# Ten mask selects and seven weight loads get another place in the order of a fused attention, gated-FFN and mixture kernel

## The chip, the cores and the metric

The kernel runs on one core of a Trainium2 chip. The metric is the device time in microseconds (us); three runs of the kernel before gave a median of 881.71 us (881.21 to 882.33).

The engines run beside each other, each through its own fixed list of instructions: PE multiplies matrices, DVE and POOL work on whole tiles element by element, ACT applies functions and copies, SP only issues transfers. ACT and POOL issue some transfers as well.

## The reference

Three stages follow each other: a linear attention whose per-channel decay is a complex number, a gated feed-forward layer, and a mixture of eight experts of which each token takes one.

```python
# 1. per batch (4) and head (8), over t = 0..767, 48 channels
S_re, S_im = ar*S_re - ai*S_im + outer(k[t], v[t]), ar*S_im + ai*S_re
y[t] = q[t] @ S_re                  # ar, ai: a_re, a_im scaled to a magnitude of at most 0.999
# 2. all 3072 tokens, 384 features
x = ((y @ w_a) * (y @ w_b)) @ w_out                 # 384 -> 1536 -> 384
# 3. experts, 384 -> 1024 -> 384
e = argmax(x @ w_gate);  out = softmax(x @ w_gate)[e] * (relu(x @ w1[e]) @ w2[e])
```

## The kernel before, in words

**Blocks.** The 3072 tokens are cut into 12 blocks of 256 tokens, three to a batch, each of two chunks of 128. For a block, ACT, DVE and POOL first work out the decays: magnitude, phase, running products and the scaled `q` and `k` (tiles `A`, `Bt`, `X`, `q`, `k`). The first block does this in two halves of 128 tokens; POOL multiplies `Bt<-im` (L1305) for each half, DVE the other parts. Transfers called turns (L1390) then bring the results into the layout that PE wants, `kT` from `Bt` and `k`, `qT` from `A` and `q`. For the first block there are 12 turns to a chunk: those of `kT` stand in SP's list, those of `qT` in ACT's. From the second block on a block has twelve, and all stand in SP's.

**Products of a chunk.** PE forms the scores (`sc_p`, L1449), DVE multiplies them with a mask into `sm` (L1458), PE transposes the keys (`kn_p`, L1463), forms `y_p` (L1498) and the state's growth (`kv_p`, L1518), and DVE carries the state on (`T`, L1524). Then the gated layer works on the block: the first block in plain fp32 (`ab_p`, L1038, the gate's product `g`, L1049 and L1052, and `o`, L1044), the later ones in three products of high and low parts (L1030, L1076), which are most of PE's work.

**Masks.** `masks` holds four planes of 128x128. Plane 0 is the causal mask and serves the blocks 0 to 2. Planes 1 to 3 are the same mask shifted by 32, 64 and 96 rows; ten selects on POOL (L1186) make them, and blocks 3 to 11 read all four planes.

**Weights.** The weights of the gated layer come as pairs of 32-bit words of 64-bit numbers, in 12 groups (0 to 11) of three loads each: `w_a`, `w_b` (L915) and `w_out` (L913), 384 KB each, into `raw` tiles. ACT (L934) and DVE (L937, L940) turn a group into fp32 tiles `a`. Of `w_out`, PE transposes each group (`wt_p`, L962), ACT copies that (L966), PE multiplies it with the gate weights of the experts (`wg_p`, L972) and ACT copies the result to the group's tile (L975). Later each group is split into high and low parts (L1002, L1008, L995, and transfers on POOL's queue, L998).

**Order.** Most of this is given to a planner (`Plan`). `add` takes an engine, an estimated duration, what the operation reads and writes, a due time `at`, and a time `early` before which it is not placed. A table `TIMES` shifts the due times of a kind of operation; that of the loads is among them. `run` then places the operations one after the other, by the engine that is free first and the smallest due time among what is ready, and this fixes each engine's list for good. What is written before the planner's work stands ahead of it in each list: the ten selects are written there. A transfer is modelled with a limit of eight that are under way. Between DVE and POOL the planner lets operations added with `alone=True` exclude each other. `conv` adds the loads and conversions of a group, `attn` a block's attention.

Of the kernel before, what the change touches and what calls it, by code (L numbers as in the profile page):

```python
# [12 lines left out]
ALU = mybir.AluOpType  # L13
AX = mybir.AxisListType
BF16 = mybir.dt.bfloat16
H, D, C, BT = 8, 48, 128, 256
HP = 64
STRIP = 32
SWAP, KEPT = 3, 2
# [92 lines left out]
    'high': (-35, 1),  # L112
    ('pre', 3, 0, 1): (-137.9, 1),
}
MAX_TAN, MIN_DECAY = 1.5, 1e-17
PT_NAMES = ("A", "Bt", "Cc", "F")
MAGIC = 12582912.0
# [240 lines left out]
def on(engine, n, psum=False, fast=False, bias=False):  # L358

    if engine == "DVE":  # L360
        return 0.147 + n * (0.00053 if fast else 0.00105)
    if engine == "ACT":
        return (0.165 if psum else 0.209) + 0.00081 * n + 0.092 * bias
    return 0.23 + 0.0021 * n
# [120 lines left out]
def fast(tc, q, k, v, a_re, a_im, w_a, w_b, w_out, w_gate, w1, w2, out, dram, x2d):  # L485

    nc = tc.nc
# [3 lines left out]
    with ExitStack() as mctx, ExitStack() as ctx:  # L491
# [10 lines left out]
        scores, phase, turns = [], [0], [0, 0]  # L502
# [10 lines left out]
        masks = ab.tile([128, 4, C], BF16, name="masks")  # L513
# [364 lines left out]
        P = Plan({"sc": 3, "s1": 3 - KEPT})  # L878
# [16 lines left out]
        def loaded(i):  # L895
            return LOAD[0] + LOAD[1] * i if i < LOAD[2] else LOAD[3] + LOAD[4] * (i - LOAD[2])

        def conv(i, f, nm, at):

            K = {}  # L900
            n, m = SIZE[nm], 768 if nm == "ab" else 384
# [39 lines left out]

            one = None
            for x in range(m // 384):
                t = loaded(i + x)
                one = P.add("SP", 0.5, load(x), kind="load", r=[("made", f)] if x else [], w=[mine[x]] + ([("made", f)] if nm == "ab" and not x else []) if nm == "ab" else mine, at=t, early=t, size=393, soft=one)
            done = ("A32", nm, f)
            if nm in BY_TAIL and f >= BY_TAIL[nm]:
# [29 lines left out]
            t = P.add("PE", 0.45, turned, kind="fold", r=[slot], w=[("wt_p", f)], at=at + 2, take="sc")  # L977
# [202 lines left out]
        for t in vrot:  # L1180
            nc.gpsimd.memset(t[:, 0::2, :, 0:HP - D], 0.0)
            nc.gpsimd.memset(t[:, 1, :, D:HP], 0.0)
        for r in range(1, 4):
            n = STRIP * (1 + (r == 2))
            for a in range(0, C, n):
                nc.gpsimd.affine_select(out=masks[a:a + n, r], in_=masks[a:a + n, r], pattern=[[1, C]], compare_op=ALU.is_ge, fill=0.0, base=-((a - r * STRIP) % C), channel_multiplier=-1)  # L1186

        def emptied(i):
            scores.append(bank([128, 4, C], "scores"))
# [234 lines left out]
        def attn(j, t0, t1):  # L1424
# [5 lines left out]
            def add(e, weight, f, r, w, **kw):  # L1430
                todo.append((e, weight, f, r, w, kw))
# [5 lines left out]
            for c in range(2):  # L1437
# [96 lines left out]
                def at_(f, *a):  # L1534
                    return lambda: f(*a)

                if j >= SWAP:
# [19 lines left out]
                        if j + 1 < NB:  # L1557
                            todo.append(("v", 0, None, (), (), {}))
                    for hg in range(2):
                        add("DVE", on("DVE", 512), at_(mask, hg), [("scores", hg % KEPT)], [("sm", hg)], alone=False)  # L1560
                    if not last:
                        for hg in range(2):
                            add("PE", 0.3, at_(kn, hg), qk + [("kT", c), "kept"], [("kn_p", j, c, hg)], take=ring(j))
# [15 lines left out]
                else:  # L1579
                    for hg in range(2):  # L1580
                        if j < SWAP:
                            add("PE", 0.9, at_(sc, hg), qk + [("kT", c), ("qT", c)], [("sc_p", j, c, hg)], take="sc")
                            add("DVE", on("DVE", 512), at_(mask, hg), [("sc_p", j, c, hg), "banks"], [("sm", hg)], give=True, alone=False)
                        else:
                            p_ = ("scores", hg % KEPT)
                            add("PE", 0.64, at_(sc, hg), qk + [("kT", c), ("qT", c)], [p_])
                            add("DVE", on("DVE", 512), at_(mask, hg), [p_], [("sm", hg)], alone=False)
                    if not last:
                        for hg in range(2):
                            add("PE", 0.33, at_(kn, hg), qk + [("kT", c), "kept"], [("kn_p", j, c, hg)], take=ring(j))  # L1590
# [14 lines left out]
            for i, (e, weight, f, r, w, kw) in enumerate(todo):  # L1605
                at = t0 + (t1 - t0) * i / len(todo)
# [32 lines left out]
        list(h1)  # L1639
        prefill()  # L1640
        attn(0, ATT[0], ATT[0] + 12)
        units = [x for f in range(NF) for x in ((3 * f, f, "ab"), (3 * f + 2, f, "o"))]
        for i, f, nm in units:
            conv(i, f, nm, CONV[0] + CONV[1] * i)
# [8 lines left out]
        for j in range(1, NB):  # L1653
# [12 lines left out]
            at = lo + 14  # L1666
# [94 lines left out]
```

## Time and profile before

| | |
|---|---|
| median of the runs | 881.71 us (881.21 to 882.33) |
| profiled execution | 881.96 us, of which the span of the instructions is 880.0 us |
| PE, weight loads beside it | 833.7 us busy (95%), 803.0 us |
| DVE, ACT, POOL | 565.0, 486.6 and 291.6 us busy |
| last chain of waits | PE 82% of the span, issue 8%, DVE 3%, DMA 3%, POOL 2%, ACT 1% |

The profiled execution's time is that of the whole run; the span goes from its first instruction to its last. The busy time of an engine is the sum over its instructions, so a share is an average over stages in which different engines set the pace. A timeline lists the instructions of one engine with start, duration and, in brackets, how long the engine had been idle before and whose end it had waited for. "SPq" and "ACTq" are the instructions by which SP and ACT issue transfers; their duration holds the time for which the issue was held up. The chain of waits is followed back from the last instruction to what released it, step by step.

### The profile page before, as it was taken

To read this page: it belongs to the slowest core of one execution; us is meant where nothing else is said; L and a number is where in the kernel's file an instruction comes from. 1 tells how busy PE (TensorE), PEld (TensorE's weight loads), DVE (VectorE), ACT (ScalarE), POOL (GpSimd) and SP (SyncE) were. 2 spreads that over 40 slices of the span, in tenths; PEclk is the share of its full clock that TensorE was granted. 3 is DMA by queue.
4 is the path that set the end of the run, shared out by engine and by line. 5 is a ranking of instruction groups with operands and counts; after the bars stand their busy time and mean duration, and the time that the engine had idled before them with its cause. 6 is when DMAs were issued, how large, how long until landed. Compare 5 with 4: busy or idle time off the path is not lost.

```text
span 880.0 us, 22475 instructions
## 1 busy us (share of the span) xinstructions
PE 833.7 (95%) x9050; PEld 803.0 (91%) x9050; DVE 565.0 (64%) x1218; ACT 486.6 (55%) x923; POOL 291.6 (33%) x295
## 2 busy tenths in 40 slices
PE   0399999999999999999999999999999999999997
PEld 0288699999999999999999999999999999999996
DVE  6889997766757577594948485535653654555541
ACT  6597878666576556565556465224542544444441
POOL 4100201422555544536363545222033323324111
PEclk9999999999999999999999999999999999999999
DMA  9886743362535362737464551523433553454410
GB/s 260 251 243 216 188 100 111 65 150 46 148 63 143 84 194 57 210 83 203 99 185 110 135 144 53 121 86 106 134 93 121 174 166 115 156 160 137 157 60 25
DMA packets 144255, 117.70 MB, mean 134 GB/s; under 512 B 51036, under 2 KB 138282, under 8 KB 144143
## 3 DMA queue, kind: packets, MB, share of 16 engines
q1 hardware_dynamic: 137071, 103.27, 42.6%
q0 software_dynamic: 5344, 12.12, 4.9%
q8 instruction: 73, 1.20, 0.6%
q10 hardware_dynamic: 1728, 0.79, 0.4%
q14 instruction: 39, 0.32, 0.1%
HBM read 85.13 MB, written 10.61 MB: 109 GB/s over the span
## 4 chain that ended last, share of the span: by engine, by line
PE 82%; issue 8%; DVE 3%; DMA 3%; POOL 2%; ACT 1%; SPq 0%; POOLq 0%; ACTq 0%
PE ab_p L1030 31%; PE o L1076 16%; PE o L843 9%; PE h_p L811 9%; PE y_p L1498 5%; PE scores L1454 2%; PE kn_p L1463 2%; PE sc_p L1449 2%; PE ab_p L1038 2%; PE kv_p L1518 2%; PE o L1044 1%; PE tn_p L788 1%; POOL out_dram L854 1%; DVE a L937 1%; DMA raw<-in_moe_w_b_dram 1%
## 5 line engine op out<-in xcount | busy, mean ns | idle before, releaser
L1030 PE MATMUL ab_p<-xH,wabH 128*128 128x256 f32 x792 | 223.4, 282 | 0.5 <-issue 0.5
L1030 PE MATMUL ab_p<-xH,wL 128*128 128x256 f32 x792 | 221.3, 279 | 0.0
L1030 PE MATMUL ab_p<-xL,wabH 128*128 128x256 f32 x792 | 221.2, 279 | 0.0
L1030 PEld LDWEIGHTS ab_p<-xH,wabH 128*128 128x128 f32 x792 | 149.9, 189 | 0.4
L1030 PEld LDWEIGHTS ab_p<-xL,wabH 128*128 128x128 f32 x792 | 148.8, 188 | 0.5 <-issue 0.4
L1030 PEld LDWEIGHTS ab_p<-xH,wL 128*128 128x128 f32 x792 | 149.2, 188 | 0.0
L1067 POOL TENSOR_TENSOR gL<-g,gH 128x256 fp32r<-128x256 f32 x96 | 80.9, 843 | 166.8 <-ACT gH L1063 154.8
L1059 DVE TENSOR_TENSOR g<-g,ab_p 128x256 f32<-128x256 f32 x132 | 55.1, 417 | 116.3 <-ACT g L1056 116.1
L1056 ACT COPY g<-ab_p 128x256 f32<-128x256 f32 x132 | 48.9, 370 | 120.8 <-PE ab_p L1030 112.6
L1076 PE MATMUL o<-woH,gH 128*128 128x392 f32 x264 | 93.8, 355 | 0.0
L1076 PE MATMUL o<-woH,gL 128*128 128x392 f32 x264 | 90.0, 341 | 0.0
L1076 PE MATMUL o<-wL,gH 128*128 128x392 f32 x264 | 89.7, 340 | 0.0
L843 PE MATMUL o<-w2H,h 128*128 128x384 f32 (+3 forms) x312 | 86.4, 340 | 0.0
L1063 ACT ACTIVATE gH<-g 128x256 fp32r<-128x256 f32 x132 | 54.6, 413 | 43.8 <-DVE g L1059 33.7
L811 PE MATMUL h_p<-sH,w1H 128*128 128x256 f32 (+6 forms) x240 | 77.2, 322 | 0.0
L811 PE MATMUL h_p<-sH,w1L 128*128 128x256 f32 (+6 forms) x240 | 77.0, 321 | 0.0
L811 PE MATMUL h_p<-sL,w1H 128*128 128x256 f32 (+6 forms) x240 | 76.8, 320 | 0.0
L854 POOL DMA_INDIRECT out_dram<-ye,ids x29 | 30.5, 1050 | 112.5 <-ACT ye L853 103.8
L822 DVE SCALAR_TENSOR_TENSOR h<-h_p,h 128x384 fp32r<-128x384 f32 (+1 forms) x48 | 26.7, 556 | 62.4 <-ACT h L820 62.2
L820 ACT ACTIVATE h<-h_p 128x384 fp32r<-128x384 f32 (+4 forms) x48 | 24.5, 511 | 76.4 <-PE h_p L811 76.4
L843 PE MATMUL o<-w2L,h 128*128 128x384 f32 (+3 forms) x168 | 56.7, 338 | 0.0
L843 PEld LDWEIGHTS o<-w2H,h 128*128 128x128 f32 (+3 forms) x312 | 56.3, 185 | 0.5
(216 smaller groups left out, 1947.0 us busy)
## 6 DMA issues: line engine op xcount, KB each, us to landing
raw<-in_moe_w_dram SPq DMA_DIRECT2D x64, 384.0 KB, 3.3
x2d<-x SPq DMA_DIRECT2D x24, 196.0 KB, 2.7
q<-in_q_dram SPq DMA_DIRECT2D x24, 192.0 KB, 4.2
v<-in_v_dram SPq DMA_DIRECT2D x24, 192.0 KB, 3.4
raw<-in_moe_w_a_dram SPq DMA_DIRECT2D x12, 384.0 KB, 4.8
raw<-in_moe_w_b_dram SPq DMA_DIRECT2D x12, 384.0 KB, 4.5
raw<-in_moe_w_out_dram SPq DMA_DIRECT2D x12, 384.0 KB, 5.3
ck<-in_moe_w_a_dram SPq DMA_DIRECT2D x12, 384.0 KB, 5.0
```

Source lines behind the costliest of these rows:

```text
L811: nc.tensor.matmul(out=t, lhsT=lh[:, o:o + 128], rhs=rh[:, kk], start=n == 0, stop=n == 8)
L820: nc.scalar.activation(out=hH, in_=t, func=ACTF.Relu)
L822: nc.vector.scalar_tensor_tensor(out=hL, in0=t[:, 0:main], scalar=0.0, in1=hH[:, 0:main].bitcast(F32), op0=ALU.max, op1=ALU.subtract)
L843: nc.tensor.matmul(out=G["o", c], lhsT=lh, rhs=rh, start=f == 0 and n == 0, stop=f == NH - 1 and n == len(ops) - 1)
L854: d = nc.gpsimd.indirect_dma_start(out, bass.IndirectOffsetOnAxis(ap=ids[0:r, c:c + 1], axis=0), y[0:r], None, bounds_check=NT - 1, oob_is ...
L1030: nc.tensor.matmul(out=t[:, i], lhsT=lh[:, kk * 128:(kk + 1) * 128], rhs=rh[:, kk], start=n == 0, stop=n == 8)
L1056: nc.scalar.copy(out=G["g", j, f], in_=G["ab", j, f][:, 0])
L1059: nc.vector.tensor_tensor(out=G["g", j, f], in0=G["g", j, f], in1=G["ab", j, f][:, 1], op=ALU.mult)
L1063: nc.scalar.activation(out=G["H", j, f], in_=G["g", j, f], func=ACTF.Copy)
L1067: eng.tensor_tensor(out=G["L", j, f], in0=G["g", j, f], in1=G["H", j, f].bitcast(F32), op=ALU.subtract)
L1076: nc.tensor.matmul(out=G["o", j, c], lhsT=lh[:, c * C:(c + 1) * C], rhs=rh, start=f == first and n == 0, stop=f == last and n == 2)
L1498: nc.tensor.matmul(out=t[q4 * 32:q4 * 32 + 32, kk], lhsT=a, rhs=b, start=f0, stop=f1)
```

## The change

The ten selects become operations of the planner, due and not placed before its time 44, and the masks of the scores now read a mark ("strips") that the selects write. They are added behind the first block's attention, so a mask of the first block doesn't wait for them; those of the later ones do. They are added with `alone=False`. And a load with number 15 or above (three numbers to a group, so from the sixth group on) is not placed before the later of its old due time and 57.2, in the loads' own count of time, which the table then shifts.

```diff
+MASKS = 44.0
+HELD = (15, 57.2)
...
             for x in range(m // 384):
-                t = loaded(i + x)
+                t = loaded(i + x) if i < HELD[0] else max(loaded(i + x), HELD[1])
                 one = P.add("SP", 0.5, load(x), kind="load", r=..., w=..., at=t, early=t, size=393, soft=one)
...
-        for r in range(1, 4):
-            n = STRIP * (1 + (r == 2))
-            for a in range(0, C, n):
-                nc.gpsimd.affine_select(out=masks[a:a + n, r], in_=masks[a:a + n, r], pattern=[[1, C]], compare_op=ALU.is_ge, fill=0.0, base=-((a - r * STRIP) % C), channel_multiplier=-1)
+
+        def strip_masks():
+            for r in range(1, 4):
+                n = STRIP * (1 + (r == 2))
+                for a in range(0, C, n):
+                    def f(r=r, n=n, a=a):
+                        nc.gpsimd.affine_select(out=masks[a:a + n, r], in_=masks[a:a + n, r], pattern=[[1, C]], compare_op=ALU.is_ge, fill=0.0, base=-((a - r * STRIP) % C), channel_multiplier=-1)
+                    P.add("POOL", 0.33, f, w=["strips"], at=MASKS, early=MASKS, alone=False)
...
-                        add("DVE", on("DVE", 512), at_(mask, hg), [("scores", hg % KEPT)], [("sm", hg)], alone=False)
+                        add("DVE", on("DVE", 512), at_(mask, hg), [("scores", hg % KEPT), "strips"], [("sm", hg)], alone=False)
...
-                            add("DVE", on("DVE", 512), at_(mask, hg), [p_], [("sm", hg)], alone=False)
+                            add("DVE", on("DVE", 512), at_(mask, hg), [p_, "strips"], [("sm", hg)], alone=False)
...
         attn(0, ATT[0], ATT[0] + 12)
+        strip_masks()
```

Since the planner orders everything anew, more moves than what the diff names. Line numbers after the change are two to six higher.

SP's list around the first block's turns, before; `raw` with `w_a` is the sixth group's first load, the first `kT<-Bt` and `kT<-k` are of the first chunk, the next two of the second:

```order
L1390 DMA kT<-Bt 16x8x128 x3
L915 DMA raw<-in_moe_w_a_dram 128x3x256
L1390 DMA kT<-k 16x8x128 x3
L1390 DMA kT<-Bt 16x8x128 x3
L1390 DMA kT<-k 16x8x128 x3
L915 DMA raw<-in_moe_w_b_dram 128x3x256
L913 DMA raw<-in_moe_w_out_dram 128x768
```

The same place in SP's list after the change:

```order
L1396 DMA kT<-Bt 16x8x128 x3
L1396 DMA kT<-k 16x8x128 x3
L1396 DMA kT<-Bt 16x8x128 x3
L1396 DMA kT<-k 16x8x128 x3
L917 DMA raw<-in_moe_w_a_dram 128x3x256
L917 DMA raw<-in_moe_w_b_dram 128x3x256
L915 DMA raw<-in_moe_w_out_dram 128x768
```

The sixth group's first load has moved from among the turns to behind them, straight ahead of its sisters.

PE's list from the second transpose of the weights to the end of the first chunk, before; the numbers are those of the weight tiles:

```order
L962 MATMUL wt_p<-ident,a_294 128x128 x3
L972 MATMUL wg_p<-wg,wt 32x8 x12
L962 MATMUL wt_p<-ident,a_327 128x128 x3
L972 MATMUL wg_p<-wg,wt 32x8 x12
L1449 MATMUL sc_p<-qT,kT 128x128 x8
L1463 MATMUL kn_p<-ident,kT 128x96 x8
L1498 MATMUL y_p<-sm,v_164 32x128 x16
L1518 MATMUL kv_p<-v_164,kn 32x48 x24
L1038 MATMUL ab_p<-x,a_274 128x128 x6
L1038 MATMUL ab_p<-x,a_287 128x128 x6
L962 MATMUL wt_p<-ident,a_547 128x128 x3
L1449 MATMUL sc_p<-qT,kT 128x128 x4
```

The same place in PE's list after the change:

```order
L964 MATMUL wt_p<-ident,a_284 128x128 x3
L974 MATMUL wg_p<-wg,wt 32x8 x12
L964 MATMUL wt_p<-ident,a_317 128x128 x3
L1455 MATMUL sc_p<-qT,kT 128x128 x8
L974 MATMUL wg_p<-wg,wt 32x8 x12
L1469 MATMUL kn_p<-ident,kT 128x96 x8
L1504 MATMUL y_p<-sm,v_164 32x128 x16
L1524 MATMUL kv_p<-v_164,kn 32x48 x24
L1455 MATMUL sc_p<-qT,kT 128x128 x4
L1040 MATMUL ab_p<-x,a_264 128x128 x6
L1040 MATMUL ab_p<-x,a_277 128x128 x6
```

The third product with the gate weights now stands behind the first chunk's scores, and half of the second chunk's scores ahead of the first `ab_p`.

POOL's list from its last fill to its first transfer, before:

```order
L1182 MEMSET vr_171 128x2x16
L1186 AFFINE_SELECT masks<-masks 32x128 x4
L1186 AFFINE_SELECT masks<-masks 64x128 x2
L1186 AFFINE_SELECT masks<-masks 32x128 x4
L1305 TENSOR_TENSOR Bt<-im 128x3x128 x2
L1281 TENSOR_TENSOR k<-k,Bt 128x3x128 x2
L1379 TENSOR_TENSOR Bt<-k,X 128x3x128 x2
L1281 TENSOR_TENSOR Bt<-A,Bt 128x768
L998 DMA wL<-a_894 128x768
```

The same place in POOL's list after the change:

```order
L1184 MEMSET vr_171 128x2x16
L1311 TENSOR_TENSOR Bt<-im 128x3x128 x2
L1287 TENSOR_TENSOR k<-k,Bt 128x3x128 x2
L1385 TENSOR_TENSOR Bt<-k,X 128x3x128 x2
L1191 AFFINE_SELECT masks<-masks 32x128
L1287 TENSOR_TENSOR Bt<-A,Bt 128x768
L1191 AFFINE_SELECT masks<-masks 32x128 x3
L1191 AFFINE_SELECT masks<-masks 64x128 x2
L1191 AFFINE_SELECT masks<-masks 32x128 x4
L1000 DMA wL<-a_882 128x768
```

One select now stands behind the first block's preparation and nine behind the square `Bt<-A,Bt` of the second block. In SP's list at the second block's turns, where before all three loads of the eleventh and of the twelfth group stand ahead of the twelve turns, there now stand the eleventh's `w_out` and the twelfth's `w_a` and `w_b` behind the first and the second of the three `kT<-k`, and the twelfth's `w_out` ahead of the last three turns.

## Rows read from the trace of the kernel before

**Rows 1.** The page: busy time, its share of the span, instructions.

```profile
PE 833.7 (95%) x9050; PEld 803.0 (91%) x9050; DVE 565.0 (64%) x1218; ACT 486.6 (55%) x923; POOL 291.6 (33%) x295
```

**Rows 2.** The chain of waits, to the first scores: start, duration, what.

```profile
7.20 0.30 POOL masks L1186
7.57 0.84 POOL Bt L1305
...
32.88 4.80 DMA raw<-in_moe_w_a_dram
37.69 1.92 DMA qT<-q
39.61 0.47 ACT wt L966
40.13 0.51 PE wg_p L972 x24
40.66 3.75 PE sc_p L1449 x16
```

**Rows 3.** Windows: length, busy PE, PEld, DVE, ACT, POOL; clock, DMA share, GB/s.

```profile
10.00:20.00 10.00, 0.00 (x0) 0.00 (x0) 9.90 (x30) 9.30 (x22) 0.51 (x1) 1.00 1.08 308
41.00:96.00 55.00, 54.99 (x615) 46.45 (x615) 47.60 (x83) 43.23 (x78) 2.89 (x2) 1.00 0.76 226
48.40:118.30 69.90, 68.73 (x881) 56.03 (x880) 67.71 (x117) 58.72 (x109) 6.51 (x6) 1.00 0.68 190
```

**Rows 4.** POOL's timeline: start, duration, instruction, idle before and its releaser.

```profile
4.07 3.42 POOL L1186 TENSOR_SCALAR_AFFINE_SELECT masks<-masks 32x128 bf16<-32x128 bf16 x10
7.57 0.83 POOL L1305 TENSOR_TENSOR Bt<-im 128x384 f32<-128x384 f32 x1
8.73 0.95 POOL L1305 TENSOR_TENSOR Bt<-im 128x384 f32<-128x384 f32 x1 [0.33 <-DMA im<-in_a_im_dram]
46.44 1.73 POOL L1281 TENSOR_TENSOR Bt<-A,Bt 128x768 f32<-128x768 f32 x1 [11.41 <-DMA raw<-in_moe_w_out_dram]
```

**Rows 5.** ACT's timeline and that of its issues (ACTq).

```profile
20.71 0.96 ACT L934 ACTIVATE a<-raw 128x768 f32<-128x768 uint32 x1 [0.38 <-DMA raw<-in_moe_w_b_dram]
26.61 0.51 ACT L1362 ACTIVATE X<-X 128x384 f32<-128x384 f32 x1
34.76 1.28 ACT L1286 ACT_TABLE_LOAD   x1 [0.53 <-issue]
39.60 0.48 ACT L966 COPY wt<-wt_p 128x384 f32<-128x384 f32 x1 [3.55 <-DMA qT<-q]
40.31 3.03 ACTq L1390 DMA_DIRECT2D qT<-q  x3
...
84.11 0.93 ACT L934 ACTIVATE a<-raw 128x768 f32<-128x768 uint32 x1
```

**Rows 6.** DVE's timeline.

```profile
8.91 1.18 DVE L1311 SCALAR_TENSOR_TENSOR X<-X,re 128x384 f32<-128x384 f32 x1
13.06 0.55 DVE L1311 SCALAR_TENSOR_TENSOR X<-X,re 128x384 f32<-128x384 f32 x1
27.71 0.55 DVE L1363 SCALAR_TENSOR_TENSOR X<-X 128x384 f32<-128x384 f32 x1
47.32 0.55 DVE L1524 SCALAR_TENSOR_TENSOR T<-kv_p,qT 96x384 f32<-96x384 f32 x1 [2.18 <-DMA qT<-q]
84.94 0.95 DVE L1379 TENSOR_TENSOR k<-k,X 128x768 f32<-128x768 f32 x1
97.23 0.56 DVE L940 SCALAR_TENSOR_TENSOR a<-raw,a 128x384 uint32<-128x384 uint32 x1
```

**Rows 7.** All instructions of DVE's line L1524: shortest, median, longest in ns.

```profile
L1524 DVE SCALAR_TENSOR_TENSOR T<-kv_p,qT x4: 543/549/554, 47.3 to 469.9; 96x384 f32<-96x384 f32 x4
```

**Rows 8.** PE's timeline.

```profile
38.33 0.87 PE L962 MATMUL wt_p<-ident,a 128*128 128x128 f32 x3 [6.98 <-DVE a L940]
97.01 0.38 PE L972 MATMUL wg_p<-wg,wt 128*32 128x8 f32 x24 [0.50 <-ACT wt L966]
97.94 0.52 PE L962 MATMUL wt_p<-ident,a 128*128 128x128 f32 x3 [0.55 <-DVE a L940]
```

**Rows 9.** SP's timeline: issues of transfers, with the time they were held.

```profile
35.74 3.45 SPq L1390 DMA_DIRECT2D kT<-Bt  x3
79.83 0.48 SPq L915 DMA_DIRECT2D raw<-in_moe_w_b_dram  x1
87.72 1.85 SPq L1390 DMA_DIRECT2D kT<-k  x3
```

## The prediction

> **What bounds the kernel now.** I read the page's busy times first: PE works 833.7 of 880.0 us [rows 1], so a change can only pay by letting PE start earlier or wait less. 46.3 us are left, and PE's scores of the first chunk begin at 40.66 [rows 2]; almost all of PE's idle time lies ahead of them. Hence the second view, the chain of waits up to there [rows 2]: it passes the last of POOL's selects (7.20), POOL's `Bt<-im` (7.57), later a weight load of 4.80 us from 32.88 that stands between turns, the last turns of the first chunk (37.69), ACT's copy of the transposed weights (39.61), their product with the gate weights (40.13, 0.51 us) and the scores. Both things that the change moves stand on this chain. The third view is the windows behind it [rows 3]: from 41 to 96 PE is busy 54.99 of 55.00 us, so a lead that PE has at 41 is one that it still has later, if DVE keeps up; from 48.40 to 118.30 DVE is busy 67.71 of 69.90 us, with 2.19 us to spare. There DVE and PE are both at their limit, and whatever DVE loses above that spare comes back as a wait of PE.
>
> **The selects leave the front.** The ten take POOL from 4.07 to 7.49 [rows 4], and `Bt<-im` of the first half comes right behind them without waiting for its data. Without them it starts when the data land, so up to 3.4 us earlier. The second half's `Bt<-im` still waits for its own transfer until 8.73 [rows 4], and DVE and ACT are busy 9.90 and 9.30 of the 10 us from 10 to 20 [rows 3], so the two halves together gain less than one does. What ends it is ACT: at 20.71 it waits 0.38 us for a weight load to land [rows 5], in a window in which the DMA engines are as full as they get (share 1.08) [rows 3], so that landing doesn't move. From there ACT has a closed row of work until the function at 26.61, which ends at 27.12 [rows 5]. DVE's next step on it starts at 27.71 [rows 6]. So of all that is gained ahead, at most 27.71 - 27.12 = 0.59 us reaches the turns. I take the middle, 0.3.
>
> **The load leaves the turns.** In the rows before, the last `qT<-q` of the first chunk is released at 37.69, when the load's 4.80 us are over [rows 2]. With the load behind the turns this chain is gone. Late next is the third transpose of weights, which waits for DVE's conversion and runs from 38.33 for 0.87 us [rows 8]: 39.20, or 38.65 if all of the 0.55 to 0.59 from the front arrives. Behind it PE's list now has the scores at once, so they start 1.46 to 2.0 us ahead of 40.66. But the third product with the gate weights, 0.51 us [rows 2], is still to be done, now behind the scores: the lead of what follows is 0.95 to 1.5 us. I take 1.2. Two things hide under the scores' 3.75 us: ACT's table load (1.28 us at 34.76), now behind the copy, and the copy itself, now behind all six turns of the second chunk. If those turns were held on ACT's queue as before, until 40.31 + 3.03 = 43.34 [rows 5], the copy (0.48) would end near 43.8, over a us behind the scores' end near 42.7, with the transposes of the keys queued behind the product on PE: that would eat the lead. Since the hold of SP's second `kT<-Bt` (3.45 us) [rows 9] falls with the load, I don't expect that; 0 is the lower end of the term.
>
> What does the lead do later? DVE waits for the first chunk's products, 2.18 us at 47.32 for instance [rows 6], so it is ahead as much as PE is, and then both run at their limit as before. The work ahead of the stretch's end is the same. So I carry 1.2 us through, with 0 to 1.5 as its bounds.
>
> **The selects come back.** One runs ahead of POOL's square of the second block and nine right behind it, at the place where that square ends, 46.44 + 1.73 = 48.17 [rows 4]. POOL is free there and the masks that read the planes come much later, so POOL itself pays nothing. But DVE begins its full stretch at 48.40. Nine selects at the old pitch of 0.34 are 3.08 us. No row shows a select beside work of DVE, so I bound it. From above: DVE's product at 8.91, beside POOL's `Bt<-im`, took 1.18 us and the same one at 13.06, alone, 0.55 [rows 6]; 0.63 lost over the 0.77 us in which both were up to 9.68 makes 0.82 for each us, so 2.5 us for nine. From below: `T` at 47.32 ran wholly beside POOL's square [rows 4, 6], and the four of its kind take 543 to 554 ns [rows 7]: nothing lost. A select has one input of 32 or 64 rows where POOL's product has two of 128, and the stretch has DVE work of both sorts, so I take 0.6, nearer to the lower row; the ends are 0 and 2.5, and 3.08 if each select took its whole pitch from DVE.
>
> The Trainium skill (SBUF — State Buffer, Who interferes with whom) states that a DVE instruction with two inputs in SBUF contends with a GpSimd instruction that reads SBUF, that one with a single such input does not, and that the side that comes first keeps the shared ports for its whole instruction. The two rows agree with it in kind: 1.18 against 0.55 us, and 549 ns unchanged. A select reads SBUF, so by the rule nearly all of its time would fall on the conversions of that stretch; this is the third rival below.
>
> **The other held loads.** Groups seven to ten have loads due later too, but SP's order among them is the same, and they are issued behind the turns of the first block as before. The turn order of the second block changes; I cost this at nothing in the likeliest case, because DVE's order moves with it, and give it a rival.
>
> **The sum**, against the profiled execution's own time of 881.96 us: -1.2 for PE's lead, +0.6 for the selects, so 881.36. The median of the runs is 0.25 under that execution, so the forecast on the median's scale is 881.1 us. A measurement of this kernel can tell about 0.2% (1.76 us) from no change; under 879.95 counts as faster, over 883.47 as slower.
>
> **Rivals.**
>
> *The lead grows on its way (faster).* The selects cost DVE nothing, as with `T`, the lead is 1.5 and PE's two waits behind the full stretch, 0.50 at 97.01 for ACT's copy and 0.55 at 97.94 for DVE's last conversion [rows 8], go as well, since the conversions are done earlier. -1.5 - 1.05 = -2.55: 879.2; with the whole 2.0 us of the scores' lead and a wait or two more, down to 878.2. For it: DVE has 2.19 us of slack [rows 3], which can swallow the selects. Against it: the sixth group's loads start later than before, not earlier.
>
> *Late loads of the last group (slower).* Before, the twelfth group's `w_b` was issued at 79.83 [rows 9] and ACT worked on it at 84.11 [rows 5], 4.3 us later. Now it stands behind the second `kT<-k`, which cannot go before DVE's `k<-k,X`, over at 84.94 + 0.95 = 85.89 [rows 6]. The third of them was still being issued at 87.72 + 1.85 [rows 9]. So `w_b` goes out at 86.5 to 88 and lands at 91 to 92.5, 7 to 8 us later than before. If ACT's list is waiting for it, with copies for PE queued behind, the last conversion (97.23 + 0.56) [rows 6] slips by 2 to 3 us and PE's wait at 97.94 grows by as much: 881.1 + 2.9 = 884.0. It decides if the landing comes after about 94 less the conversion's own 3 us, or if ACT's list has the conversion too early. Against it: DVE's products for the turns now stand earlier relative to the conversions, by about a group.
>
> *The selects lock DVE out (slower).* Each takes its pitch from DVE: 3.08 in place of 0.6, so 881.71 - 1.2 + 3.08 = 883.6. It needs DVE instructions of the kind seen at 8.91 beside nearly each of the nine, and DVE's slack already spent.
>
> **How the numbers follow.** The forecast has 0.42: its own range is 879.8 to 883.2 (the lead between 0.3 and 1.5, the selects between 0 and 1.8); 0.03 of it lies on the faster side and 0.03 on the slower. The faster rival has 0.38 (0.34 faster, 0.04 within), the late loads 0.12 (0.11 slower), the lock 0.08 (0.06 slower). Faster 0.37, within 0.2% 0.43, slower 0.20. The range goes to 878.0 below, the faster rival's end, and to 884.1 above, past both slower ones, and leaves about 2 in 10 outside.
>
> **What would show it.** Right: POOL's `Bt<-im` starts by 6 us; the scores start between 38.6 and 39.3, with the third gate product (0.5 us) behind them and no wait on PE ahead of the keys' transposes; nine selects between 46 and 52, with DVE's conversions beside them longer by some tenths in all; PE's instructions around 90 some 0.6 us earlier. Wrong: scores at 40 or later (another transfer holds them), a wait on PE of over a us at the third gate product, a span of DVE at 48 to 52 that is 2 us longer, or a wait on PE at 90 to 100 for a conversion of the twelfth group. If the end moves by more than PE's lead at 50 does, the difference was made by the new order later, which I cost at nothing.

## The result: slower by 0.7%, by waits far behind the edits

The changed kernel takes 888.23 us (median of 14 runs, 883.8 to 894.63), the kernel before beside it 882.11 (14 runs): a ratio of 1.0067, interval 1.0051 to 1.0083, so about 6 us slower. The forecast was 881.1, between 878.0 and 884.1, and most likely no change to be measured. The profiled execution took 883.80 us with a span of 881.9 and is the shortest of the 14, so it shows less of the loss than the others have. Busy times on its page, to be read beside [rows 1]:

```profile
PE 835.8 (95%) x9050; PEld 804.3 (91%) x9050; DVE 566.5 (64%) x1218; ACT 486.3 (55%) x923; POOL 293.1 (33%) x295
```

PE is 2.1 us busier with the same instructions, so for a part of the time it works at a lower rate. The chain of waits to the first scores, where [rows 2] had the selects, the load and the last turns:

```profile
35.97 1.35 DVE a L942 x2
37.45 0.87 PE wt_p L964 x3
38.32 1.72 PE sc_p L1455 x8
```

The load and the turn are gone from it, DVE's conversion and the third transpose bound the scores, and they start at 38.12 to 38.32 in place of 40.66. Up to here the forecast's mechanism held. POOL's timeline, for [rows 4]:

```profile
5.22 0.83 POOL L1311 TENSOR_TENSOR Bt<-im 128x384 f32<-128x384 f32 x1 [1.12 <-DMA im<-in_a_im_dram]
...
45.28 1.73 POOL L1287 TENSOR_TENSOR Bt<-A,Bt 128x768 f32<-128x768 f32 x1 [10.66 <-DMA k<-in_k_dram]
47.09 6.88 POOL L1191 TENSOR_SCALAR_AFFINE_SELECT masks<-masks 32x128 bf16<-32x128 bf16 x9
```

The nine selects take 6.88 us where ten took 3.42. DVE's timeline beside them shows who paid:

```profile
46.51 0.92 DVE L939 SCALAR_TENSOR_TENSOR a<-raw,a 128x384 uint32<-128x384 uint32 x1
...
50.74 1.04 DVE L939 SCALAR_TENSOR_TENSOR a<-raw,a 128x768 uint32<-128x768 uint32 x1
51.71 1.04 DVE L1287 TENSOR_TENSOR X<-X,im 128x768 f32<-128x768 f32 x1
...
53.73 0.64 DVE L939 SCALAR_TENSOR_TENSOR a<-raw,a 128x384 uint32<-128x384 uint32 x1
...
54.97 0.55 DVE L942 SCALAR_TENSOR_TENSOR a<-raw,a 128x384 uint32<-128x384 uint32 x1
```

A conversion of 384 columns takes 0.55 us alone (the last line, behind the selects); here one takes 0.64 and one 0.92, but the latter ran beside POOL's square until 47.01 and only then beside the first select. Instructions of 768 columns take 1.04 for 0.95. So DVE lost 0.3 us beside the selects, or 0.7 with the whole of the 0.92 counted. POOL lost 3.8, and POOL had nothing to do. Two of the nine selects ran beside `sm` (49.27), which reads only its mask from SBUF (the scores lie in PSUM), and took 0.29 us each, as before. The other seven took 0.49 to 1.01 us, and each ended 0.14 to 0.16 us behind a DVE instruction with two inputs in SBUF that had begun ahead of it.

Where, then, is the time lost? PE's waits by what ended them (sum, count, longest), and windows of the page's kind (columns as in [rows 3]):

```profile
PE wt_p L964 <- DVE a L942: 33.4, 3, 26.0
PE rk_p L672 <- DVE oh L649: 2.9, 2, 2.1
PE wg_p L974 <- ACT wt L968: 1.2, 2, 0.7
PE ab_p L1040 <- DVE a L942: 0.8, 1, 0.8
PE sc_p L1455 <- DMA k<-in_k_dram: 0.5, 1, 0.5
```

```profile
90.00:100.00 10.00, 9.06 (x141) 7.16 (x141) 9.06 (x15) 9.04 (x17) 1.15 (x1) 1.00 0.93 217
500.00:510.00 10.00, 7.91 (x115) 7.64 (x114) 9.62 (x22) 5.07 (x9) 3.34 (x3) 0.93 0.81 244
510.00:520.00 10.00, 10.00 (x218) 9.66 (x216) 9.83 (x25) 6.06 (x12) 4.13 (x4) 0.90 0.14 44
```

I counted the products `ab_p` in both traces and compared the starts of those with the same number. The changed kernel leads by 1.56 us at 155, 1.76 at 214, 2.73 at 336 and still 1.69 at 494. At 535 it is 2.06 us behind, and this holds to the end. Between 494 and 535 there is a wait of 2.10 us, and two windows have a granted clock of 0.93 and 0.90. The trace shows one stretch at the lower level, 1.2 GHz for 2.4, from 508.58 to 511.99: 0.07 + 0.10 of 10 us, 1.7 us of work. That makes 3.8 us together, where 3.75 were lost.

This execution was a lucky one in two ways. Ahead of 40 to 48 us PE's products go at about half of their later rate, and the trace's record of the clock begins with an entry at the higher level at the moment when that ends (last section): at 40.95 here, at 44.89 in the profile of the kernel before. So a part of the lead is the clock's. And the other three profiles of the changed kernel, taken with the experiments below, lose more between 70 and 102. The lead over that one profile of the kernel before, in us (below 0 is behind), at products `ab_p` of the same number, named by their start in the kernel before:

| profile | first entry of the clock | at 70.5 | 102.5 | 494.0 | 535.0 |
|---|---|---|---|---|---|
| changed kernel, the first profile | 40.95 | 3.02 | 0.61 | 1.69 | -2.06 |
| changed kernel, a1_after | 47.59 | 0.24 | -4.65 | -3.38 | -6.15 |
| changed kernel, a2_after | 45.61 | 1.06 | -3.35 | -2.47 | -5.88 |
| changed kernel, a3_after | 40.84 | 3.32 | -3.38 | -2.18 | -5.51 |
| both edits without a new plan, e5_edits_in_place | 43.72 | 0.55 | 0.70 | 0.64 | 0.64 |

So there are two places of loss: the first between 70 and 102, where 2.4 to 6.7 us of lead go (some 2 come back by 336), the second between 494 and 535, where 2.8 to 3.8 go. I take the second up first, as it is the larger in the first profile.

What PE waits for at the second place is `rk_p`, the ranking of a block's tokens by expert. PE's timeline:

```profile
504.78 1.32 PE L1460 MATMUL scores<-qT,kT 96*32 96x128 f32 x64
508.19 0.18 PE L672 MATMUL rk_p<-oh,strict 128*128 128x8 bf16 x1 [2.10 <-DVE oh L649]
```

and DVE's, which makes `oh`, the choice of the expert (`span<-ck` reads a second copy of the weights and checks their range; it has nothing to do with the tokens):

```profile
496.86 0.42 DVE L1061 TENSOR_TENSOR g<-g,ab_p 128x256 f32<-128x256 f32 x1 [2.77 <-ACT g L1058]
500.24 1.01 DVE L602 TENSOR_REDUCE span<-ck 128x1 f32<-128x384 f32 x2 [2.95 <-DMA ck<-in_moe_w_a_dram]
501.17 0.95 DVE L1317 SCALAR_TENSOR_TENSOR X<-X,re 128x768 f32<-128x768 f32 x1
...
505.88 1.16 DVE L646 TENSOR_TENSOR sj<-lgt,rm 128x16 f32<-128x16 f32 x1
507.08 0.65 DVE L647 SCALAR_TENSOR_TENSOR rr<-sj,ebias 128x16 f32<-128x16 f32 x1
507.76 0.17 DVE L648 TENSOR_REDUCE rm<-rr 128x2 f32<-128x16 f32 x1
507.96 0.17 DVE L649 TENSOR_TENSOR oh<-ebias,rm 128x16 bf16<-128x16 f32 x1
```

DVE stands 2.95 us for a load that SP issued only at 496.06:

```profile
496.06 0.58 SPq L599 DMA_DIRECT2D ck<-in_moe_w_a_dram  x1
```

In the kernel before, the same load went out at 490.23, its reductions ran at 498.89 without a wait, and `rk_p` ran at 506.34 without one. SP's, DVE's and PE's timelines of the kernel before:

```profile
490.23 0.53 SPq L597 DMA_DIRECT2D ck<-in_moe_w_a_dram  x1
```

```profile
498.89 1.00 DVE L600 TENSOR_REDUCE span<-ck 128x1 f32<-128x384 f32 x2
...
504.05 0.18 DVE L644 TENSOR_TENSOR sj<-lgt,rm 128x16 f32<-128x16 f32 x1
```

```profile
506.34 0.18 PE L670 MATMUL rk_p<-oh,strict 128*128 128x8 bf16 x1
```

The reductions stand ahead of the choice in both orders, but the load for them now goes out behind two groups of turns. Behind the check DVE has five instructions, 3.6 us, of the next block's preparation and a check of its decays (`ok`), now ahead of the choice. And two tiny steps of the choice, `sj` and `rr`, take 1.16 and 0.65 us beside POOL's products, where before they took 0.18 each:

```profile
505.29 1.72 POOL L1287 TENSOR_TENSOR A<-A,Bt 128x768 f32<-128x768 f32 x1 [1.36 <-ACT Bt L1283]
506.98 0.72 POOL L1069 TENSOR_TENSOR gL<-g,gH 128x256 fp32r<-128x256 f32 x1
```

Nobody edited any of these instructions: the planner placed them anew.

### The profile page after: what moved, and what is told of

It reads as the page before. It is cut to its first block, busy times and chain, and to the rows that moved or that the text cites. A ratio compares the mean times of both kernels' runs of the same rounds, so it can differ in the third digit from the quotient of the medians.

```text
span 881.9 us, 22478 instructions
## 1 busy us (share of the span) xinstructions
PE 835.8 (95%) x9050; PEld 804.3 (91%) x9050; DVE 566.5 (64%) x1218; ACT 486.3 (55%) x923; POOL 293.1 (33%) x295
## 4 chain that ended last, share of the span: by engine, by line
PE 80%; issue 8%; DVE 4%; DMA 3%; POOL 2%; ACT 1%; SPq 1%; POOLq 0%; ACTq 0%; DVEq 0%
PE ab_p L1032 30%; PE o L1078 16%; PE o L845 9%; PE h_p L813 9%; PE y_p L1504 5%; PE ab_p L1040 3%; PE scores L1460 2%; PE o L1046 2%; PE kn_p L1469 2%; PE kv_p L1524 1%; PE sc_p L1455 1%; DMA raw<-in_moe_w_out_dram 1%; PE tn_p L790 1%; POOL out_dram L856 1%; DMA raw<-in_moe_w_b_dram 1%
## 5 line engine op out<-in xcount | busy, mean ns | idle before, releaser
L1069 POOL TENSOR_TENSOR gL<-g,gH 128x256 fp32r<-128x256 f32 x96 | 77.0, 802 | 170.6 <-ACT gH L1065 162.0
```

The costliest lines, as they stand in the source:

```text
L1069: eng.tensor_tensor(out=G["L", j, f], in0=G["g", j, f], in1=G["H", j, f].bitcast(F32), op=ALU.subtract)
```

## The experiments

Each was compared with the kernel before, run beside it on the same chip. The median of the kernel before was 882.1 to 882.7 us in four of these comparisons and 887.0 and 887.1 in two. Chip 10 stands in both groups, so this isn't the chip alone, and only ratios within a comparison are set against each other. The changed kernel itself gave 1.0047 to 1.0077 in four comparisons. The diffs show the lines that matter, abridged. Where an edit is said to be made in the finished lists, the planner's order was computed as usual and then single instructions were moved by hand.

**Each half alone, planned anew.**

```diff
 e1_selects_only
-HELD = (15, 57.2)
+HELD = (99, 57.2)          # no load has such a number
 e2_held_only: the kernel before, and
+                t = loaded(i + x) if i < HELD[0] else max(loaded(i + x), HELD[1])
```

> Only the selects go to the planner; the loads keep their old due times. Theory (the loss has one place: the ranking's products on PE near 508 us wait for DVE, which had waited for a late load of the weights' check, and the granted clock falls behind that wait): the end depends on what the planner makes of that place, not on the selects. The lead at PE's first scores is then up to 0.6 us, and if the place keeps the order of before, the time is 881 to 883. Rival (the selects beside DVE's conversions, or what they push, cost the time): slower than before by 3 us or more, 885 to 890, with the loss already seen in PE's starts between 50 and 130 us.

> Only the loads are held; the selects stay in the preamble. Theory: the scores start 1.5 to 2.0 us earlier than before by the load alone, and that lead holds until about 300; the end is 879.5 to 881 if no wait for the ranking comes up near 500, and 884 or more, with a granted clock under 0.999, if one does. Rival (the later loads of the sixth and the last groups cost the time): slower than before by 2 us or more with the loss between 80 and 130 us.

Measured: the selects alone 0.9993 (0.9980 to 1.0006), the held loads alone 1.0077 (1.0050 to 1.0104). So the selects cost nothing, and the loss comes with the held loads and the plan that follows from them. In the profile of the second PE waits 1.9 us for the choice at 515, with a granted clock of 0.83 in the window from 510 to 520, and is busy 7.25 us only between 90 and 100. Both theories had named one of these places; both places are there.

**The check moved, and a delay put in.**

```diff
 e3_check_behind: the changed kernel, in the finished lists
+        out[k:k] = late        # the two reductions of check load 25, behind the ranking's choice
 e4_before_with_delay: the kernel before
+                    for _ in range(10):
+                        nc.vector.tensor_tensor(out=pad, in0=zeros, in1=zeros, op=ALU.mult)
                     pick()
```

> The changed kernel with one edit: the two reductions of the check's 25th load (the pair that waited 2.95 us for its load) stand behind the ranking's choice in DVE's list, not ahead of it. Theory: DVE doesn't stand still there, the choice is ready some 3 us earlier, PE's wait of 2.1 us at 508 and the fall of the clock behind it go, and the time is 878.5 to 880.5, 2 to 3 us under before, with a spread between executions as small as before's. Rival (the wait is a symptom, the loss lies in the order elsewhere or in POOL's work beside the ranking): 883 to 888, as wide as before the edit.

> The kernel before with ten extra products of zeros on DVE (about 3.4 us, one scratch tile) ahead of the ranking's choice of the same block. Nothing is left out of the computation. Theory: PE's ranking products wait about 2 us there, the clock falls for some us, and the time rises by 3 to 7 us over before, with a granted clock of 0.99 to 0.998 and a wide spread. Rival (a wait of that length costs just its length, the rest came from elsewhere): plus 1.5 to 2.5 us, the clock at 0.999, and a narrow spread.

With the check behind: 1.0041 (1.0019 to 1.0063), not the 2 to 3 us under before that I expected. The wait at this choice is gone (the one of 0.6 us left for `rk_p` is at the choice ahead of it, at 464), but PE was busy only 7.18 us from 90 to 100, so another place was left. The changed kernel didn't run beside this one, so what the move is worth is read further below. With the delay: 1.0051 (1.0030 to 1.0071), 4.6 us by the medians. PE's timeline and windows of that run:

```profile
512.69 0.18 PE L672 MATMUL rk_p<-oh,strict 128*128 128x8 bf16 x1 [2.75 <-DVE oh L649]
```

```profile
510.00:520.00 10.00, 7.31 (x99) 7.05 (x99) 6.74 (x22) 4.81 (x9) 4.78 (x5) 0.83 0.67 162
```

A wait of 2.75 us and 0.17 of 10 us of clock make 4.5 us. One late choice is enough for a loss of the size of the changed kernel's, and more than a third of it is the clock behind the wait.

**The edits without a new plan.**

```diff
 e6_load_in_place: the kernel before, in the finished lists
+        out[k:k] = held        # the sixth group's first load, behind the first block's turns
 e5_edits_in_place: as e6, and
+        out.insert(k, selects) # all ten, behind POOL's Bt<-A,Bt of the second block
 b1_before, a1_after: unchanged
```

> The kernel before, unchanged, for a profile on this chip. Expected: the same waits of PE as in the profile shown (0.5 to 0.7 us each at 97, 98, 135 and 318), no wait for the ranking's choice over 1 us, and on this chip short further pauses of PE that no engine ends.

> The changed kernel, unchanged, in five rounds beside the kernel before on one chip, and a second profile. Theory (two places: the last group's loads behind the second block's turns, and the ranking's choice behind a late load of the check): 0.5 to 0.9% slower than before; PE's first scores 1.5 to 2.5 us earlier than before; that lead falls to between 0 and 1 us by 110, and at 508 PE waits 1.5 us or more with a granted clock under 0.95 in the window behind. Rival (the loss is spread over the run): the difference to before grows evenly from 130 to 620 us.

> The kernel before with the two edits done by hand in its finished lists, without planning anew: the sixth group's first load moves behind the first block's turns, the ten selects behind POOL's square of the second block. Every other instruction keeps its place. Theory (the edits help at the front and the new order of the rest costs the time): 1 to 2.5 us faster than before, PE's first scores 1 to 2 us earlier, no wait over 1 us for the ranking. Rival (the edits themselves cost the time, by the selects beside DVE or by the later load): no faster, or slower by 2 us or more.

> The kernel before with the one load moved by hand behind the first block's turns, the selects where they were. Theory: PE's first scores 1 to 1.6 us earlier than before, the end 0.5 to 1.5 us earlier, so most of the front's gain is the load's. Rival (the selects' place makes the lead): less than 0.5 us of lead and no measurable change.

The changed kernel gave 1.0047 (1.0030 to 1.0064), both edits in place 0.9998 (0.9987 to 1.0010), the load alone 1.0004 (0.9994 to 1.0014). So the edits alone neither cost nor bring what can be measured (the interval leaves room for a gain of 1.1 us), and the new order of the rest costs all of the loss; that they would bring 1 to 2.5 us was wrong. Their scores, with both edits and with the load alone, start at 40.00 and 40.28, only 0.4 and 0.1 us ahead of the unchanged kernel's 40.42 on that chip, because the product with the gate weights still stands ahead of them and the transposes' copy bounds it. The second profile of the changed kernel shows the first place plainly:

```profile
90.00:100.00 10.00, 6.81 (x57) 5.35 (x55) 6.14 (x10) 4.90 (x11) 1.15 (x1) 1.00 0.89 234
```

against the kernel before on the same chip (one execution, 885.20 us, without a wait of over 0.8 us for a choice):

```profile
90.00:100.00 10.00, 8.34 (x85) 6.22 (x84) 7.97 (x13) 8.30 (x15) 2.10 (x3) 1.00 0.87 215
```

**Half of each order.** Both plans are computed; one gives every engine's list for what is planned before 130 us, the other the rest.

```diff
 e7_old_then_new / e8_new_then_old, in run()
+        one, two = old, new                  # e8: new, old; old is that of e5
+        cut = [k for k, o in enumerate(one) if o[0] >= 130.0][0]
+        out = one[:cut] + [o for o in two if o[1] not in there]
 e9_old_then_new_check: as e7, with the reductions moved as in e3
 e10_in_place_fold: as e5, and
+        out.insert(pe, fold)                 # the third gate product, behind the first scores
```

> Every engine's list is that of the run with both edits in place (the old order) for all that was planned before 130 us, and the changed kernel's from there. Theory of two places: the loss at 70 to 110 us is gone, that at 450 to 520 stays: PE waits 1.5 us or more for the ranking's choice at about 508, and the time is 0.2 to 0.5% over before. Rival (all of the loss comes from the second block's loads, and the later waits only follow from it): no wait over 1 us at 508, time within 0.2% of before.

> The other way round: the changed kernel's order for all that was planned before 130 us, and the old one from there. Theory of two places: PE waits about 3 us between 70 and 110, 1 to 2 us more than before, none over 1 us at 508; with the lead of 2 us at the front the time is within 0.2% of before or up to 0.3% over it. Rival (the first place alone): 0.4% or more over before, as the changed kernel.

> As the run with the old order to 130 us and the new one behind, with one more edit: the two reductions of the check's 25th load stand behind the ranking's choice. Theory: the wait at 508 falls under 0.7 us and the time comes down by 0.15 to 0.4% against the run without this edit, to within 0.2% of before. Rival (the wait for the late load isn't what costs; POOL's work beside the ranking or the order of 450 to 500 does): no difference between the two runs.

> The run with both edits in place and, in addition, PE's third product with the gate weights moved by hand behind the first chunk's scores, as in the changed kernel; nothing else moves. Theory: the scores start about 1 us earlier than with the edits in place, and the time is 0.1 to 0.2% under before. Rival (PE's lead at the front is lost on the way to 110 us, where DVE sets the pace): within 0.1% of before, as with the edits in place.

The new order behind 130 us alone: 1.0064 (1.0048 to 1.0081), over the 0.2 to 0.5% expected, with a wait of 1.8 us for the choice. With the check moved: 1.0027 (1.0013 to 1.0041). So this one pair of reductions costs about 0.37%, some 3 us, and the wait falls to nothing. At the seam itself a wait of 1.7 us for a split of weights comes in, in both, which neither whole order has; in the profile with the check moved the clock is at the lower level behind it, from 137.31 to 140.73. So both ratios hold something of the seam. The new order ahead of 130 us alone: 1.0043 (1.0022 to 1.0064), as the rival had it and more than I had expected, with no wait over 1 us at the choice. The two halves make more than the whole: the seam adds to one of them, and a part of one may be hidden behind the other where both are there; no run tells these apart. With the third product moved too, the edits in place give 0.9994 (0.9981 to 1.0007): the scores start at 38.32, and a gain of 1 us would still lie within the interval.

**Undoing the first place.** By the trace, it is the chain of the last weights. SP's, ACT's and PE's timelines of the changed kernel's first profile:

```profile
85.90 0.52 SPq L917 DMA_DIRECT2D raw<-in_moe_w_b_dram  x1
```

```profile
90.70 0.90 ACT L936 ACTIVATE a<-raw 128x768 f32<-128x768 uint32 x1 [2.16 <-DMA raw<-in_moe_w_b_dram]
```

```profile
90.41 2.83 PE L1040 MATMUL ab_p<-x,a 128*128 128x256 f32 x12 [0.84 <-DVE a L942]
94.87 1.13 PE L1455 MATMUL sc_p<-qT,kT 96*128 96x128 f32 x8 [0.53 <-DMA k<-in_k_dram]
```

The twelfth group's `w_b` goes out 6.1 us later than before [rows 9] and ACT's conversion of it starts 6.6 us later [rows 5].

```diff
 e11_loads_first: the changed kernel, in the finished lists
+        move([("head", "o", 7), ("head", "ab", 8)], ahead=...)    # two conversions on DVE ahead of the four products for the turns
+        move([("raw", 32), ("raw", 33), ("raw", 34)], ahead=...)  # three loads ahead of the second block's turns
 e12_both_undone: as e11, and the check's reductions as in e3
 e13_loads_first_act: as e11, and
+        move([Bt<-im of the third block], behind=("tail", "ab", 11))   # on ACT
 e14_both_undone_act: as e13, and the check's reductions as in e3
 a2_after, a3_after: the changed kernel
```

> The changed kernel, unchanged, as the measure for the two runs beside it on the same chip: 0.4 to 0.7% over before, with waits of PE of 2 to 3.5 us in all between 70 and 110 us and of 1.5 us or more at about 508.

> The changed kernel with the first place undone by hand: two of DVE's conversions stand ahead of the four products for the second block's turns again, and the eleventh group's third load and the twelfth's first two ahead of those turns. Theory: the twelfth group's w_b goes out 4 us earlier, PE's waits between 70 and 110 fall by 1 us or more to what the kernel before has (about 1.2), and the time by 0.15 to 0.35% against the changed kernel; the wait at 508 stays. Rival (the turns of the second block, now later, cost as much): no difference to the changed kernel.

> As the run before, and the two reductions of the check's 25th load moved behind the ranking's choice as well. Theory of two places: within 0.2% of the kernel before, 0.4 to 0.6% under the changed kernel. Rival (there are more places of the kind in the new order): still 0.25% or more over before.

On one chip: the changed kernel 1.0077 (1.0062 to 1.0092), the loads first 1.0093 (1.0076 to 1.0110), both 1.0059 (1.0041 to 1.0077). My edit missed its aim: PE now waits 4.2 and 5.0 us near 96, since ACT's list still had the third block's `Bt<-im` ahead of the conversions:

```profile
92.90 0.84 ACT L1324 ACTIVATE Bt<-im 128x768 f32<-128x768 f32 x1 [6.41 <-DMA kT<-Bt]
```

It overwrites what the turn reads, and the turn had gone behind three loads.

> The changed kernel, unchanged, as the measure on the same chip: 0.4 to 0.8% over before.

> As the run with the loads ahead of the second block's turns, and ACT's Bt<-im of the third block behind the conversion of the twelfth group's w_a and w_b. Theory (the conversions' chain makes the first place): ACT no longer stands for a turn, PE's waits between 70 and 110 us fall under 2 us, and the time is 0.15% or more under the changed kernel beside it. Rival (that place costs what the transfers take in any order): PE waits 3 us or more there and the time is that of the changed kernel.

> As the run before, with the two reductions of the check's 25th load behind the ranking's choice. Theory of two places: 0.4% or more under the changed kernel beside it, within 0.25% of before. Rival (further places in the new order): 0.3% or more over before.

On another chip: the changed kernel 1.0060 (1.0040 to 1.0081), loads first with ACT's part 1.0063 (1.0046 to 1.0080), both 1.0034 (1.0018 to 1.0049). In the profile of the loads first, the first place is all but gone (window 90 to 100, the changed kernel and then the loads first):

```profile
90.00:100.00 10.00, 6.98 (x76) 5.55 (x75) 6.18 (x10) 6.71 (x13) 1.15 (x1) 0.77 0.92 213
```

```profile
90.00:100.00 10.00, 8.77 (x114) 6.77 (x113) 8.94 (x15) 8.08 (x16) 1.15 (x1) 1.00 0.88 233
```

Yet the median didn't move, against my theory. The profiled execution (0.998, 885.00 us) is the shortest of the six; the others have a mean granted clock of 0.992 to 0.996, those of the kernel before 0.998 to 0.999. The mean over all six is 0.9945, against 0.9984 for the kernel before and 0.9963 for the changed kernel: by this estimate the clock alone makes 3.4 of the 5.6 us over before, for the changed kernel 1.9 of 5.3. Behind which waits it fell in those executions is not shown. With both undone the first place is not gone: PE waits 2.07 us at 97 for a load of `k`. So this run doesn't say what would be left without both places. The check's pair was worth 0.29% here, 0.34% on the chip before and 0.37% in the halves.

## Why the prediction was wrong

**The step that failed** is "So I carry 1.2 us through", with "the work ahead of the stretch's end is the same" ahead of it, and the new order behind it "cost at nothing". The lead itself was of the right size: at 70 us and at the same clock it is 1.2 to 1.4 us. This is an estimate from the table: for a first entry at 44.89, as in the kernel before, its rows give 1.4; for 46.88, as in that kernel's other profile, which is 0.66 behind the first one there, they give 0.5, so 1.2 more. It did not last. What took it, and 5 to 9 us of lead in all, was an order of instructions that the planner made over again: 2.4 to 6.7 us went between 70 and 102, and 2.8 to 3.8 between 494 and 535, 450 us behind the edits. That the order is the cause is shown: the same edits without a new plan give 0.9998, the new order's two halves 1.0043 and 1.0064. My own last sentence of what would make it wrong named this case, but it had no chance and no price. It could have had one: the order of both kernels was at hand, and DVE's list there has the five instructions of the preparation and its check ahead of the choice that PE waits for, and SP's has the check's load behind two groups of turns.

**The selects at the front.** Forecast 0.3 us at the turns with 0.59 as the upper bound; the first turn of `kT` went out at 29.93, 0.97 us ahead of 30.90. The bound rested on a landing that "doesn't move", read from a window that ends at 20, ahead of that wait. It moved: ACT goes on at 20.32 in place of 20.71, and 0.39 more than 0.59 is what was gained. This is on the way to the scores too, for the third transpose begins 0.88 us earlier, at 37.45.

**The load out of the turns.** Right: the chain through it vanished, the third transpose bound the scores. In the first profile they lead by 2.5 us, over the 1.46 to 2.0 worked out, mostly because the front gave more. That 0.95 to 1.5 us would be left behind them fits the estimate of 1.2 to 1.4, but partly by luck: that PE's first products go at half rate, so that a lead there counts for half, is not in the sum. No wait on PE came at the gate product, so 0 as lower end wasn't needed.

**The selects beside DVE.** Right in size: 0.6 us taken, 0.3 to 0.7 measured. The rival in which they lock DVE out fell: POOL was the one to stand, 6.88 us for 3.08. The Trainium skill (SBUF — State Buffer, Who interferes with whom) says that issue order decides who blocks; the trace agrees, for the seven selects that took longer each ended 0.14 to 0.16 us behind a DVE instruction that had begun ahead of it. So the rule didn't say, as I read it, that the selects' time would fall on DVE: DVE had an instruction ready nearly all the time and came first.

**The late loads** had 0.12 and came true as described: `w_b` 6.1 us later, for 7 to 8 forecast, conversions late, PE waiting between 90 and 98. The price, 2.9 us, is near to what the order ahead of 130 us costs alone (0.43%, 3.8 us; 0.22 to 0.64%). That the order of DVE's list would make up for it was the wrong argument: it was what delayed the loads, since the conversions that free the buffers stand behind the four products. This last part is argued from the traces; undoing it by hand took the waits away in one profile, but not the time.

**The sum** has a slip: the forecast's own range begins at 879.8, but its terms give 881.71 - 1.5 = 880.2. It decided nothing.

**What stays open.** Moving the check gives back 0.3 to 0.4%. Of the rest, 0.3% was there in the last run, in which the check was moved but the first place was not quite undone; its mean clock is below that of the kernel before (0.9966 against 0.9984, some 1.7 of its 3.0 us by the same estimate). How that 0.3% divides between the first place, the clock and places that I haven't found isn't shown.

## What to carry to other kernels

An edit to a planner's input is two edits: the one meant, and a new order of everything behind it. Test them apart, by moving the instructions in the finished order, and by taking half of either order; then read the new order at the places where the critical engine waits for a chain of small steps. A wait of 2 to 3 us on a saturated PE can cost more than its length, because the clock may fall behind it: here 4.6 us for one of 2.75. And one pair of profiles is one pair of executions: see when the clock rose in each before a lead is read from them.

## What the runs showed of the hardware that was not expected

PE's first products go at about half their later rate, and when that ends doesn't depend on when PE began. The scores' products of 128 columns start 213 ns apart at first and 112 later. In all 20 profiles the change comes where the trace's record of the granted clock has its first entry, at the higher level (2.4 GHz), between 40.84 and 47.81 us. Ahead of that entry there is none, and the windows and the mean clock count the time as 1.00. That it is time at the lower level is read from the rate: in the stretch from 508.58 to 511.99 of the first profile, recorded at the lower level, the products `o` start 0.33 us apart, ahead of and behind it 0.18. In the first profile of the changed kernel PE began the scores at 38.12 and was at the higher rate with `kv_p`; in the second it began at 38.42 and was not:

```profile
43.66 0.86 PE L1524 MATMUL kv_p<-v,kn 128*32 128x48 f32 x48
```

```profile
45.59 1.50 PE L1524 MATMUL kv_p<-v,kn 128*32 128x48 f32 x48
```

So a lead at the first products counts for about half where the clock rises late. The changed kernel's second profile (first entry at 47.59) leads the kernel before on that chip (46.88) by 2.0 us at the scores and by 0.9 at 70. This is one reason why the edits in place, with the third product moved and the scores at 38.32, bring so little.

Waits of 1.7 to 2.75 us at the choice were followed by a granted clock of 0.83 to 0.93 in windows of 10 us in five profiles, and waits of 1.7 to 1.9 us by 1.00 in four others, so the length of the wait alone doesn't settle it. At the first place too: in one of the changed kernel's four profiles (a3_after) the clock was at the lower level from 95.45 to 102.28, behind a wait of 1.83 us; behind waits of 1.64 and 1.89 us there, in two others, it was not. The changed kernel's 14 executions spread over 10.8 us, with a mean clock from 0.990 to 0.999, and the longest are those with the lowest clock (0.990: a span of 892.6 us; 0.992: 890.7); the kernel before spread over 3.9 us.
